# Maxima rows read from PSUM, row sums and gates issued at other places, operand splits in another order, in an attention and gated-unit kernel

## Chip, core and metric

The kernel runs on one core of one Trainium2 chip. Times are device microseconds (us) of that core for one execution. Before the change three runs took 1293.97 to 1294.17 us, with a median of 1294.0.

## The reference

```python
x, g = A_x, sigmoid((A_x * gate_w).sum(-1, keepdims=True))   # 2048 tokens, D = 448
q, k, v = (x @ wqkv).reshape(B, S, 3, 16, 28) ...             # 16 heads of 28 dimensions
a = softmax(q @ k.T * 28 ** -0.5) @ v @ wo
b = (relu(x @ W_gate) * (x @ W_up)) @ W_down                  # F = 1792
return g * a + (1 - g) * b
```

Everything is float32, and the softmax subtracts the maximum of each row.

## The kernel before

**Arithmetic.** TensorE works on float32r tiles. An operand that needs more precision is split into a high part (a copy rounded to float32r: `act_high` on ScalarE, `dve_high` on VectorE) and a low part (what the rounding left, a subtraction: `low` on VectorE, `pool_low` on GpSimd, called POOL here). A product over the 448 input dimensions (three chunks of 128 and one of 64) is then a sum of 11 matmuls, the list `TERMS`: pairs of a plane of the weights (0 to 2 high, 3 to 5 low, 6 both parts of the last chunk) and a chunk of the activations (0 to 3 high, 4 to 7 low). `BY_CHUNK` and `HIGH_FIRST` are the same 11 terms in other orders; in the latter the terms with high weights come first.

**Order of the work.** The schedule is manual: every engine runs its instructions in the order in which the program issues them. Each engine's queue is in order, and so are the queues of DMA issues, those of SyncE (SP) for loads and those of POOL for stores and small reshapes. An instruction at the head of a queue that waits for a semaphore holds up what stands behind it.

**Phase 1, up to some 145 us.** X (activations, transposed) and W (the q, k, v weights) are loaded in blocks and split. `split_first` (line 234) splits weight block 0 and X_0 chunk by chunk: high part of W, high part of X, low part of W, low part of X, for chunks 0 to 3. `split_w` (220) splits a later block of 224 weight columns, which holds two units of 128-column-wide results (its view has an axis `j` of four heads), and `split_x` (266) splits a later block of 512 tokens in two pieces of two chunks. `qk(tb, c)` (300) computes one unit of Q and K: 11 matmuls, then ScalarE's high part of the result and, in the inner function `send`, VectorE's low part and a DMA of both to memory. `send` is called at once, but for the last unit, (0, 6): its `send` is kept and runs at the letter "l" of the first round. That unit's result goes into the second half of the tile `pair`, the raw first gate weights into its first half; those are split into `wg` by `split_f` ahead of the first round. `vproj` computes V and the gate logits `zt`.

**Phase 2, some 145 to 1065 us.** There are 32 rounds of eight key tiles, two for each of the 16 heads. The first of a head is called even, the second odd. A string of letters gives a round's order on TensorE (`FIRST`, `LONG`, `WIDE`, `LATE`):

- "s": a score matmul (tile `s`), and ScalarE's exponential of it into `P`; in the last three rounds two matmuls and one exponential;
- "m": two matmuls of K and Q into a PSUM pair `sm`, and VectorE's maximum over it into a column of `mx`. 32 of them give the row maxima of a head ahead of its turn;
- "x": one of the 11 terms of a gate or up unit (`gu`), "h" a last term; at its end `relu` on ScalarE or the product `h` on VectorE.

The round ends with the split of the next gate weights (`split_f`: ScalarE, POOL) and with `pv` (496), the product of the probabilities and V, 32 matmuls into a PSUM tile `po` of tag "mx", that of the `sm` pairs. The even round's `po` is copied to `os` by ScalarE, the odd round's is added to it by VectorE, and a DMA from POOL reshapes the 2048 row sums into `ls`.

An odd round (and, for head 0, one place in phase 1) begins with `smax_end(h)` (159): TensorE transposes the maxima into a PSUM tile `mt` of tag "x" (two buffers, shared with the `gu` units); ScalarE copies it to `mr` and rounds `mr` into `mh[:, 0]`; VectorE takes the low part; two DMAs issued by POOL write the two as rows 112 and 113 of `Q[h]`, where K has rows of -1, so that the score matmul subtracts the maximum.

`small_things` (554) runs at the start of a round and again behind its 16th score (with the even round's start as quarter 0, so the middle of the even round is quarter 1, the start of the odd one quarter 2). For the head before, quarter 1 issues `row_sums` (VectorE's reciprocal of `ls` into `rs`, a POOL DMA to memory, `l_d`) and `spread` (four POOL DMAs that read `l_d` back, broadcast to `rb`); quarter 2 issues `normalise` (VectorE multiplies `os` by `rb`, four POOL DMAs write `o_d`). The first round's quarter 1 issues `gates` (the sigmoid: an exponential on ScalarE, three VectorE operations).

**Phase 3.** After the last `po` the remaining gate and up units, the output projection (`wo`, with the split weights `WO`) and the down projection (`acc`, weights `WD`). `split_wo` (546) is issued between the last two rounds; `row_sums`, `spread` and `normalise` of head 15 are placed among the first gate units and down products.

## Time and profile before

| | |
|---|---|
| median of three runs | 1294.0 us |
| profiled execution | 1294.1 us, its span 1292.3 |
| TensorE matmuls (PE) | 1285.5 us busy, 99% of the span |
| weight loads (PEld) | 923.7 us, 71% |
| VectorE (DVE) | 808.6 us, 63% |
| ScalarE (ACT) | 749.2 us, 58% |
| GpSimd (POOL) | 366.9 us, 28% |
| granted TensorE clock | 0.9 or more of full speed in every fortieth of the span |

The time of an execution is a little longer than the span of its profile. PE and PEld are two rows of the same engine: the next matmul's weights are loaded while the last one runs, so a weight load that waits (its idle time is given with what ended it) is where TensorE's wait for another engine is seen. Rows of a group have the line, the engine, the operation, the tiles out and in, the count, the busy time and the mean, and then the idle time ahead of them with its releaser. Rows of the timeline and of the chain begin with the start and the length in us.

### The profile page before, as it was taken

Reading aid. Unit: us, or ns where it says so; the run is one execution under the profiler, and the core shown is the slowest. Engines: PE = TensorE matmul, PEld = TensorE weight load, DVE = VectorE, ACT = ScalarE, POOL = GpSimd, SP = SyncE. Lnnn points to the kernel's source line nnn. Section 1 sums busy time; section 2 is a strip of 40 time slices with the busy share of each in tenths; the row PEclk is TensorE's granted clock in tenths of the full one; section 3 lists DMA queues with packets and bytes.
Section 4 is the critical chain, followed back from the end, with each engine's and each line's share of the span. In section 5 each row is a group of like instructions: output and inputs, shape, how many; then the busy total and the mean of one; then the engine's idle time right before and its main releaser. Section 6 shows DMA issues by size and latency. Waiting matters only on the chain.

```text
span 1292.3 us, 17710 instructions
## 1 busy us (share of the span) xinstructions
PE 1285.5 (99%) x6687; PEld 923.7 (71%) x6687; DVE 808.6 (63%) x834; ACT 749.2 (58%) x1402; POOL 366.9 (28%) x551
## 2 busy tenths in 40 slices
PE   9999999999999999999999999999999999999998
PEld 6888766666666666666666666666666656899997
DVE  6487866666777676777766667777777212663342
ACT  5212766666667667676766666767676765322121
POOL 3222132332313222222223332313132353641020
PEclk9999999999999999999999999999999999999999
DMA  9846524151427223241535142432341224644432
GB/s 313 293 156 235 143 87 99 58 129 47 117 63 190 77 78 90 59 99 49 139 101 127 50 114 65 107 70 78 81 132 42 81 87 141 201 136 147 135 110 78
DMA packets 53565, 148.87 MB, mean 115 GB/s; under 512 B 10024, under 2 KB 17128, under 8 KB 48872
## 3 DMA queue, kind: packets, MB, share of 16 engines
q1 hardware_dynamic: 36120, 98.34, 29.1%
q0 software_dynamic: 16928, 48.93, 10.6%
q8 instruction: 53, 0.87, 0.3%
q10 hardware_dynamic: 432, 0.46, 0.1%
q14 instruction: 32, 0.26, 0.1%
HBM read 102.06 MB, written 46.02 MB: 115 GB/s over the span
## 4 chain that ended last, share of the span: by engine, by line
PE 94%; issue 2%; DMA 1%; POOL 1%; ACT 1%; DVE 0%; SPq 0%; ACTq 0%; POOLq 0%
PE gu L468 21%; PE sm L152 18%; PE po L503 16%; PE s L178 16%; PE acc L712 11%; PE qk L303 5%; PE v L321 3%; PE wo L668 3%; PE s L189 2%; DMA ls<-os 1%; POOL wg L99 1%; DMA wr<-wq 0%; PE mt L162 0%; ACT wg L90 0%; ACT WO L90 0%
## 5 line engine op out<-in xcount | busy, mean ns | idle before, releaser
L154 DVE TENSOR_REDUCE mx<-sm 128x1 f32<-128x1024 f32 x512 | 611.1, 1221 | 85.5 <-PE sm L152 85.1
L180 ACT ACTIVATE P<-s 128x512 f32<-128x512 f32 x724 | 401.3, 596 | 174.3 <-PE s L178 164.2
L468 PE MATMUL gu<-X,wg 128*128 128x512 f32 (+1 forms) x1232 | 422.3, 401 | 0.2 <-ACT wg L90 0.2
L178 PE MATMUL s<-Q,K 114*128 114x512 f32 x932 | 364.4, 398 | 0.0
L152 PE MATMUL sm<-K,Q 112*128 112x512 f32 x1024 | 322.4, 396 | 0.3 <-DVE mx L154 0.3
L468 PEld LDWEIGHTS gu<-X,wg 128*128 128x128 f32 (+1 forms) x1232 | 226.5, 189 | 63.7 <-issue 13.8
L152 PEld LDWEIGHTS sm<-K,Q 112*128 112x128 f32 x1024 | 193.5, 190 | 43.9 <-DVE mx L154 4.1
L178 PEld LDWEIGHTS s<-Q,K 114*128 114x128 f32 x932 | 176.2, 189 | 54.4 <-issue 10.1
L503 PE MATMUL po<-P,V 128*32 128x512 f32 x1600 | 181.0, 594 | 0.0
L490 POOL DMA_DIRECT2D h_d<-h x56 | 31.5, 563 | 519.5 <-DVE h L484 455.7
L99 POOL TENSOR_TENSOR wg<-wgr,wg 128x384 fp32r<-128x384 f32 x204 | 146.3, 735 | 8.1
L180 ACT ACTIVATE V<-s 128x512 f32<-128x512 f32 x208 | 115.1, 596 | 45.6 <-PE s L178 43.4
L712 PE MATMUL acc<-WD,hh 128*128 128x448 f32 x672 | 140.9, 368 | 0.0
L712 PEld LDWEIGHTS acc<-WD,hh 128*128 128x128 f32 x672 | 126.1, 188 | 12.9
L503 PEld LDWEIGHTS po<-P,V 128*32 128x32 f32 x1600 | 49.5, 110 | 111.5 <-issue 106.4
L90 ACT ACTIVATE hh<-hr 128x512 fp32r<-128x512 f32 x56 | 35.2, 631 | 119.5 <-PE acc L712 119.5
L96 DVE TENSOR_TENSOR hh<-hr,hh 128x512 fp32r<-128x512 f32 x56 | 46.1, 824 | 64.2 <-ACT hh L90 64.2
L303 PE MATMUL qk<-X,W 128*128 128x512 f32 x308 | 79.6, 399 | 0.4 <-DVE X L96 0.2
L303 PEld LDWEIGHTS qk<-X,W 128*128 128x128 f32 x308 | 58.4, 190 | 15.3 <-DVE X L96 0.7
L90 ACT ACTIVATE wg<-wgr 128x384 fp32r<-128x384 f32 x165 | 66.3, 490 | 3.8 <-DMA wgr<-wgu 2.6
L509 DVE TENSOR_TENSOR os<-po,os 128x512 f32<-128x512 f32 x16 | 11.1, 692 | 91.2 <-PE po L503 91.2
L96 DVE TENSOR_TENSOR mh<-mr,mh 16x128 fp32r<-16x128 f32 x16 | 5.9, 368 | 91.5 <-ACT mh L166 91.5
(73 smaller groups left out, 759.5 us busy)
## 6 DMA issues: line engine op xcount, KB each, us to landing
wgr<-wgu SPq DMA_DIRECT2D x55, 512.0 KB
K<-qk_d SPq DMA_DIRECT2D x64, 224.0 KB
Q<-qk_d SPq DMA_DIRECT2D x64, 224.0 KB
h_d<-h POOLq DMA_DIRECT2D x56, 256.0 KB, 2.3
hr<-h_d SPq DMA_DIRECT2D x56, 256.0 KB
qk_d<-st POOLq DMA_DIRECT2D x21, 512.0 KB, 3.7
x_d<-X POOLq DMA_DIRECT2D x6, 1024.0 KB, 5.1
X<-x_d SPq DMA_DIRECT2D x24, 256.0 KB
```

The lines of the kernel that those rows point to most:

```text
L90: nc.scalar.activation(dst, src, AF.Copy)
L96: nc.vector.tensor_tensor(dst, src, f32(high), op=OP.subtract)
L99: nc.gpsimd.tensor_tensor(dst, src, f32(high), op=OP.subtract)
L152: nc.tensor.matmul(ps[:, c, :], Q[h][:GD, u * P:(u + 1) * P], K[h % 3][:GD, k0:k0 + TB], start=True, stop=True)
L154: nc.vector.tensor_reduce(MX[h][:, 2 * u + half:2 * u + half + 1], ps, axis=AX.XY, op=OP.max)
L178: nc.tensor.matmul(ps, K[h % 3][:GD + 2, kt * P:(kt + 1) * P], Q[h][:GD + 2, j * TB:(j + 1) * TB], start=True, stop=True)
L180: nc.scalar.activation(PT[i][:, j], ps, AF.Exp, scale=SCALE)
L303: nc.tensor.matmul(ps, W[:, a, c * P:(c + 1) * P], xf(tb, b), start=(n == 0), stop=(n == NT - 1))
L321: nc.tensor.matmul(ps[:, :VC], xf(tb, b)[:, t * P:(t + 1) * P], W[:, a, 2 * D:], start=(n == 0), stop=(n == NT - 1))
L468: nc.tensor.matmul(ps, WS[i][rows, s, a], xf(i // NF, b)[rows], start=(n == 0), stop=(n == NT - 1))
L503: nc.tensor.matmul(po[32 * j:32 * j + 32], V[:, h // 4 % 2, i % NK, h % 4], p[:, j], start=(i == i0), stop=(i == i0 + ni - 1))
L712: nc.tensor.matmul(ACC[i // NF][t][:, :D], HH[i][:, a, t * P:(t + 1) * P], WD[:, f, b], start=(f == 0 and n == 0), stop=(f == NF - 1 and n ...
```

## The change

- `smax_end`: `mr` is gone. ScalarE rounds the PSUM tile `mt` directly into `mh[:, 0]`, and VectorE's low part reads PSUM too. The low part and the two POOL DMAs become a function `rest` that the caller runs: in a round behind its first "m", in the late rounds at once, in phase 1 at once.
- `split_first`: the groups are now W and X of chunk 0, W and X of chunk 1, W of chunks 2 and 3, X of chunks 2 and 3.
- `split_w`: of block 1 the columns of the first unit (`j` = 0) are split ahead of the others. The unit (0, 1) uses `HIGH_FIRST`. `split_x` takes the last two chunks of X_1 one at a time.
- `qk`: ScalarE's high part moves into `send`. That changes the order for the last unit alone, where `send` runs later than the splits of the gate weights.
- `gates` moves from the middle of the first round to the end of the second, ahead of `pv`. `row_sums` and `spread` move from the middle of the even round to the start of the odd one, `normalise` from the start of the odd round to its end, ahead of `pv`.
- `split_wo`: the high parts are made by VectorE in place of ScalarE.

```diff
@@ -160,13 +160,15 @@
 
         pt = ps_x(f"mt_{h}")
         nc.tensor.transpose(pt[:16, :P], M.pop(h), ident)
-        mr = keep.tile([16, P], F32, name=f"mr_{h}", tag="mr", bufs=1)
         mh = keep.tile([16, 2, P], F32R, name=f"mh_{h}", tag="mh", bufs=1)
-        nc.scalar.activation(mr, pt[:16, :P], AF.Copy)
-        nc.scalar.activation(mh[:, 0], mr, AF.Copy)
-        low(mh[:, 1], mr, mh[:, 0])
-        for r in range(2):
-            nc.gpsimd.dma_start(f32(Q[h])[GD + r:GD + r + 1], f32(mh)[:, r])
+        act_high(mh[:, 0], pt[:16, :P])
+
+        def rest():
+            low(mh[:, 1], pt[:16, :P], mh[:, 0])
+            for r in range(2):
+                nc.gpsimd.dma_start(f32(Q[h])[GD + r:GD + r + 1], f32(mh)[:, r])
+
+        return rest
 
     PT = {}
 
@@ -219,31 +221,48 @@
 
         def split_w(wr, c0, c1):
 
-            ways = [(W[:, :, c0:c1], wr)]
+            ways = [[(W[:, :, c0:c1], wr)]]
             if c0 < 2 * D:
                 w, r = (ap.rearrange(f"p c {n} -> p c a j d", a=2, j=4)
                         for ap, n in ((W[:, :, c0:c1], "(j a d)"), (wr, "(a j d)")))
-                ways = [(w[:, :, a], r[:, :, a]) for a in range(2)]
-            for w, r in ways:
-                act_high(w[:, 0:3], r[:, 0:3])
-                low(w[:, 3:6], r[:, 0:3], w[:, 0:3])
-            for w, r in ways:
-                act_high(w[:, 6], r[:, 3])
-                low(w[64:, 6], r[64:, 3], w[64:, 6])
+                ways = [[(w[:, :, a], r[:, :, a]) for a in range(2)]]
+
+                if c0 == 2 * GD:
+                    ways = [[(w[:, :, :, 0], r[:, :, :, 0])], [(w[:, :, a, 1:], r[:, :, a, 1:]) for a in range(2)]]
+            for way in ways:
+                for w, r in way:
+                    act_high(w[:, 0:3], r[:, 0:3])
+                    low(w[:, 3:6], r[:, 0:3], w[:, 0:3])
+                for w, r in way:
+                    act_high(w[:, 6], r[:, 3])
+                    low(w[64:, 6], r[64:, 3], w[64:, 6])
 
         def split_first(wr, xr):
 
             r = wr.rearrange("p c (a j d) -> p c a j d", a=2, j=4)
             w = W[:, :, :2 * GD].rearrange("p c (j a d) -> p c a j d", a=2, j=4)
-            for c in range(4):
-                part = xr[c // 2][2][:, c % 2:c % 2 + 1]
+
+            def weights(c):
                 act_high(w[:, c if c < 3 else 6], r[:, c])
-                act_high(X[0][0][:, c:c + 1], part)
+                yield
                 if c < 3:
                     low(w[:, 3 + c], r[:, c], w[:, c])
                 else:
                     low(w[64:, 6], r[64:, 3], w[64:, 6])
+                yield
+
+            def tokens(c):
+                part = xr[c // 2][2][:, c % 2:c % 2 + 1]
+                act_high(X[0][0][:, c:c + 1], part)
+                yield
                 low(X[0][1][:, c:c + 1], part, X[0][0][:, c:c + 1])
+                yield
+
+            for group in ((weights(0), tokens(0)), (weights(1), tokens(1)), (weights(2), weights(3)),
+                          (tokens(2), tokens(3))):
+                for _ in range(2):
+                    for part in group:
+                        next(part)
 
         def load_x(tb):
             r = []
@@ -265,8 +284,10 @@
 
         def split_x(tb, raw):
             for c0, c1, xr in raw:
-                act_high(X[tb][0][:, c0:c1], xr)
-                low(X[tb][1][:, c0:c1], xr, X[tb][0][:, c0:c1])
+
+                for a, b in ((c0, c0 + 1), (c0 + 1, c1)) if (tb, c0) == (1, 2) else ((c0, c1),):
+                    act_high(X[tb][0][:, a:b], xr[:, a - c0:b - c0])
+                    low(X[tb][1][:, a:b], xr[:, a - c0:b - c0], X[tb][0][:, a:b])
 
         def spill_x(tb, r):
             nc.gpsimd.dma_start(x_d[tb, r], f32(X[tb][r]))
@@ -303,9 +324,9 @@
                 nc.tensor.matmul(ps, W[:, a, c * P:(c + 1) * P], xf(tb, b), start=(n == 0), stop=(n == NT - 1))
                 mix(n, among)
             st = st_tile(tb, c)
-            act_high(st[:, 0], ps)
 
             def send():
+                act_high(st[:, 0], ps)
                 low(st[:, 1], ps, st[:, 0])
                 nc.gpsimd.dma_start(qk_d[:, c * P:(c + 1) * P, tb * TB:(tb + 1) * TB].rearrange("r d t -> d r t"),
                                     f32(st))
@@ -365,7 +386,7 @@
 
         x2 = load_x(2)
         w2 = load_w(2)
-        qk(0, 1)
+        qk(0, 1, HIGH_FIRST)
         split_x(2, x2)
         x3 = load_x(3)
         qk(1, 0)
@@ -420,7 +441,7 @@
             f(*a, among=among)
 
             if 0 in M and ends >= 2 * NK:
-                smax_end(0)
+                smax_end(0)()
         assert m == ahead, m
 
     def gates():
@@ -544,9 +565,9 @@
         return r[:, :, :D]
 
     def split_wo(r):
-        act_high(WO[:, 0:3], r[:, 0:3])
+        dve_high(WO[:, 0:3], r[:, 0:3])
         pool_low(WO[:, 3:6], r[:, 0:3], WO[:, 0:3])
-        act_high(WO[:, 6], r[:, 3])
+        dve_high(WO[:, 6], r[:, 3])
         pool_low(WO[64:, 6], r[64:, 3], WO[64:, 6])
 
     nxt = parts = i0 = 0
@@ -561,15 +582,11 @@
         if u in (16, 32):
             g = u // 16 + 1
             nc.sync.dma_start(V[:, g % 2], v_d[g])
-        if u == 1:
-            gates()
         if u == 2:
             pack_wo()
-        if h and q == 1:
+        if h and q == 2:
             row_sums(h - 1)
             spread(h - 1)
-        if h and q == 2:
-            normalise(h - 1)
 
     split_f(0, act_high, pool_low, (0,))
     fetch_f(1)
@@ -580,8 +597,11 @@
         todo = list(range(nxt, nxt + nu))
         nxt += nu
         small_things(i0 // 4)
+        rest = None
         if m % (2 * NK) == 0 and i0 <= NI - LEAD:
-            smax_end(m // (2 * NK) - 1)
+            rest = smax_end(m // (2 * NK) - 1)
+            if late:
+                rest()
         if late and wor is None:
             wor = load_wo()
 
@@ -603,6 +623,10 @@
             elif o == "m":
                 smax(m)
                 m += 1
+
+                if rest:
+                    rest()
+                    rest = None
             elif o == "x":
                 i, half, n = passes.pop(0)
                 if n == 0:
@@ -635,6 +659,11 @@
             parts += 1
             if parts % 2 == 0:
                 fetch_f(parts // 2 + 1)
+
+        if i0 == NK // 2:
+            gates()
+        if i0 > NK and i0 % NK:
+            normalise(i0 // NK - 1)
         pv(i0, ni)
         i0 += ni
         if late and i0 == NI - NK // 2:
```

## The prediction

> **What bounds the kernel now.** I read the page first, then the chain that ended last in order of time, then the waits, then the timeline at the places where the weight loads (PEld) waited for another engine. The page gives TensorE nearly the whole span:
>
> ```profile
> PE 1285.5 (99%) x6687; PEld 923.7 (71%) x6687; DVE 808.6 (63%) x834; ACT 749.2 (58%) x1402; POOL 366.9 (28%) x551
> ```
>
> A busy TensorE may still lose time between matmuls, so the chain matters more:
>
> ```profile
> 10.33 28.09 PE qk L303 x120
> ...
> 615.48 7.01 PE po L503 x64
> 645.18 7.01 PE po L503 x64
> 675.08 7.01 PE po L503 x64
> ...
> 767.04 7.01 PE po L503 x64
> 797.09 7.01 PE po L503 x64
> ...
> 1098.05 2.48 PE acc L712 x12
> ```
>
> Columns: start, length, what. From 10.33 us the matmuls run at 28.09/120 = 0.234 us each, and the chain stays on TensorE. The starts of the probability-times-V block (`po`) give the length of a round. 615.48 to 645.18, a first-half ("even") round, takes 29.70 us; 645.18 to 675.08, a second-half ("odd") round, which begins with the transposition of the maxima, takes 29.90; the odd round 767.04 to 797.09, one of five of a slower kind, takes 30.05. So the steady part is bound by the number of matmuls, which the change leaves alone, and it can win only the short gaps in front of single matmuls, the start before 10.33, and places where TensorE stands still for one late operation. I call the matmul's own time TensorE's floor; what follows is a list of its exceptions.
>
> **The change, part by part.** The sum is made against the profiled execution, which took 1294.1 us (span 1292.3 and 1.8 around it), 0.1 over the median of 1294.0.
>
> *Start.* Order of the first splits, first part of block 1 ahead of the rest, second unit with its high terms first, last piece of X_1 in two. Timeline of before:
>
> ```profile
> 7.50 0.69 DVE L96 TENSOR_TENSOR X<-xr,X 128x512 fp32r<-128x512 f32 x1 [0.26 <-ACT X L90]
> ...
> 8.64 0.69 DVE L96 TENSOR_TENSOR X<-xr,X 128x512 fp32r<-128x512 f32 x1
> ...
> 8.83 1.23 ACT L90 ACTIVATE W<-wr 128x336 fp32r<-128x336 f32 x4 [0.56 <-DMA wr<-wq]
> 9.35 1.42 DVE L96 TENSOR_TENSOR W<-wr,W 128x336 fp32r<-128x336 f32 x4
> 9.39 0.19 PEld L303 LDWEIGHTS qk<-X,W 128*128 128x128 f32 x1 [0.48 <-DVE X L96]
> ...
> 10.33 27.66 PEld L303 LDWEIGHTS qk<-X,W 128*128 128x128 f32 x120 [0.40 <-DVE W L96]
> ...
> 11.53 2.41 DVE L96 TENSOR_TENSOR X<-xr,X 128x1024 fp32r<-128x1024 f32 x2
> ```
>
> Before, VectorE's queue runs X chunk 2, W chunk 3, X chunk 3, and waits 0.26 us for ScalarE's part of X chunk 2. The W chunk 3 part takes about 0.45 (8.19 to 8.64). After, W chunk 3 stands ahead of both X chunks on both engines: its VectorE part fills the 0.26 wait, and X chunk 3 ends near 9.05 instead of 9.33. The first unit's last matmul starts then, not at 9.39. Block 1 lands as before (ScalarE got it at 8.83). Its first ScalarE part shrinks from 336 to 168 columns, so it ends near 9.15 instead of 9.3, and six terms with high weights now need nothing from VectorE: 6 x 0.234 = 1.4 us, in which the low part (about 0.35 after 9.2) is ready. So the second unit starts near 9.3 and runs through to 9.3 + 11 x 0.234 = 11.9; before, its second term waited until 10.33 and the unit ended at 10.33 + 10 x 0.234 = 12.7. Gain 0.8. Against it: two more operations on ScalarE and VectorE each (about 0.2 us) stand ahead of X_1, whose low parts took VectorE until 11.53 + 2.41 = 13.94. They would now end near 14.3; the third unit wants the last of them at 11.9 + 10 x 0.234 = 14.2. I take 0.1 off: **0.7**; ends 0.25 (only the first unit's part) and 0.95.
>
> *Last qk unit.* Its ScalarE high part moves behind the first split of the gate weights:
>
> ```profile
> 144.37 0.60 ACT L90 ACTIVATE pair<-qk 128x512 fp32r<-128x512 f32 x1
> ...
> 144.60 0.64 PE L178 MATMUL s<-Q,K 114*128 114x512 f32 x2
> 144.85 0.53 ACT L90 ACTIVATE wg<-pair 128x384 fp32r<-128x384 f32 x1
> ...
> 145.43 0.53 PEld L468 LDWEIGHTS gu<-X,wg 128*128 128x128 f32 x3 [0.64 <-ACT wg L90]
> 145.43 0.96 PE L468 MATMUL gu<-X,wg 128*128 128x512 f32 x3 [0.19 <-ACT wg L90]
> ...
> 146.22 0.63 PE L152 MATMUL sm<-K,Q 112*128 112x512 f32 x2
> ```
>
> ScalarE did `pair` (0.60) first, `wg` after it, and the first gate matmul waited. TensorE should have gone on at 144.60 + 2 x 0.234 = 145.07 and went on at 145.43, and lost 0.09 more on restarting (145.43 + 3 x 0.234 = 146.13, the next matmul at 146.22). Together 0.45, at an idle time of the weight loads of 0.64: below I take idle less 0.19 for what the matmuls lose. After, `wg` takes the place of `pair`, half a microsecond earlier, and the wait is gone; `pair` is late next, and only its DMA waits for that. **0.45**; low end 0, should `wg` wait for the memory it takes over.
>
> *Maxima rows from PSUM.* One of two ScalarE copies per head goes (0.25); VectorE's low part and the two POOL DMAs move behind the round's first maximum. The start of the odd round that begins when the `po` block of 767.04 ends (774.05):
>
> ```profile
> 774.61 0.25 ACT L165 ACTIVATE mr<-mt 16x128 f32<-16x128 f32 x1
> ...
> 774.89 0.31 ACT L166 ACTIVATE mh<-mr 16x128 fp32r<-16x128 f32 x1
> ...
> 775.10 2.25 ACT L180 ACTIVATE P<-s 128x512 f32<-128x512 f32 x4
> 775.23 0.42 DVE L96 TENSOR_TENSOR mh<-mr,mh 16x128 fp32r<-16x128 f32 x1 [5.92 <-ACT mh L166]
> ...
> 775.73 0.19 PEld L178 LDWEIGHTS s<-Q,K 114*128 114x128 f32 x1 [0.27 <-ACT P L180]
> ...
> 776.84 0.30 PEld L152 LDWEIGHTS sm<-K,Q 112*128 112x128 f32 x2 [0.33 <-DVE mx L154]
> ...
> 777.49 1.02 POOL L169 DMA_DIRECT2D Q<-mh  x2
> ```
>
> The first exponential starts behind `mr` and `mh`, and the third score matmul's weight load waits 0.27 for it. VectorE's queue stands for 5.92 us at `mh`, with the first maximum behind it, and the third pair of maxima matmuls waits 0.33 for that. After, `mh` starts at 774.61 and the exponential near 774.85, 0.25 earlier, which covers the 0.27 up to the normal gap; and the first maximum is reduced ahead of the low part, so its PSUM is free about 0.4 earlier, over the 0.33. PSUM of the transposition is held until the low part is done, a little over 1 us longer; the next gate unit but one wants it, 11 matmuls later. From the chain, an odd round costs 0.20 more than an even one, one of the slower kind 0.35. The transposition and its load keep some of that; I take 0.10 in each of 14 odd rounds (0.27 - 0.19 = 0.08 from the load's wait; ends 0 and 0.20) and 0.15 more in the five of the slower kind, where the maxima wait too (ends 0 and 0.15): 1.4 + 0.75 = **2.15**; ends 0 and 3.55.
>
> *Row sums, spreading, normalisation.* The same operations, half a round later each. One place shows what that is worth:
>
> ```profile
> 393.92 0.25 DVE L517 RECIPROCAL rs<-ls 128x16 f32<-128x16 f32 x1 [1.68 <-DMA ls<-os]
> ...
> 395.30 0.30 PEld L152 LDWEIGHTS sm<-K,Q 112*128 112x128 f32 x2 [0.72 <-DVE mx L154]
> ```
>
> The reciprocal waited 1.68 for a slow landing of the row sums, with the maxima behind it on VectorE, and TensorE lost 0.72 - 0.19 = 0.53. After, the transfer has half a round more. **0.53**; ends 0 and 0.53. On POOL the order changes: at the start of an odd round now stand the write of the reciprocals, a wait for it to land, four spreading DMAs, and only then the maxima rows for the next head, in place of four output DMAs of 0.51 each (as the two of 1.02 above):
>
> ```profile
> POOL rb L524 <- DMA l_d<-rs: 53.7, 15, 7.2
> ...
> POOL ls L512 <- DVE os L509: 21.8, 8, 3.3
> ```
>
> ```profile
> L528 DVE TENSOR_TENSOR os<-os,rb 128x512 f32<-128x512 f32 x16 | 13.1, 817 | 2.0 <-DMA rb<-l_d 2.0
> ```
>
> Columns of the waits: total, times, longest; of the group: busy, mean ns. The wait for that landing took 53.7/15 = 3.6 us on average, 7.2 at most. So the maxima rows, issued 3.4 us into the round (777.49 against 774.05), go near 3.4 + 0.5 + 3.6 = 7.5, at worst 11.1. The first score that needs them is the 29th of 32 in the round; with 28 scores, 26 or so gate terms and 15 pairs of maxima ahead, it comes (28 + 26 + 30) x 0.234 = 19.7 us into the round. Cost nothing; the cover is 8.5 us or more. The four output DMAs now stand ahead of the row sums' transfer at the end of an odd round. That transfer had waited for VectorE 21.8/8 = 2.7 us, more than the 2.04 of four issues, and is wanted a round later. The multiplication itself (0.82 on average) moves from among the maxima to just behind POOL's weight splits, where the 7.01 of `po` cover it.
>
> *Gates.* One small exponential and three small VectorE operations go to where both engines stand idle beside `po`. Nothing.
>
> *Output weights' high part on VectorE, and the tail:*
>
> ```profile
> 1059.19 6.04 POOL L99 TENSOR_TENSOR wg<-wgr,wg 128x384 fp32r<-128x384 f32 x8
> ...
> 1063.24 1.78 ACT L90 ACTIVATE WO<-wor 128x1344 fp32r<-128x1344 f32 x2
> ...
> 1065.99 0.30 PEld L189 LDWEIGHTS s<-Q,K 114*128 114x128 f32 x2 [1.21 <-ACT V L191]
> ...
> 1095.05 0.25 DVE L517 RECIPROCAL rs<-ls 128x16 f32<-128x16 f32 x1 [0.80 <-DMA ls<-os]
> 1095.42 0.39 DVE L93 CAST WD<-wdr 128x448 fp32r<-128x448 f32 x1
> ...
> 1096.20 1.23 POOL L99 TENSOR_TENSOR WD<-wdr,WD 128x448 fp32r<-128x448 f32 x1
> ```
>
> ScalarE's 1.78 us of WO held up the exponentials, and the scores lost 1.21 - 0.19 = **1.02**. VectorE has nothing to do there (no maxima in the last three rounds). WO has 4 x 448 columns a partition; at the 0.39 of the cast of 448 above, 1.56 us of casts. Its rival for memory is POOL:
>
> ```profile
> L93 DVE CAST WD<-wdr x14: 382/392/3841, 1095.4 to 1155.5; 128x448 fp32r<-128x448 f32 x14
> ```
>
> The same cast of 448 columns took 0.38 at least and 3.84 at most, beside POOL's own splits. So the casts and POOL's `wg` parts (6.04 us for eight, the first done by 1059.95) may delay each other by 1.56 or more. Even then the first `wg` part is there by 1061.5, while the gate matmuls begin after `po`, near 1063. I take 0; ends 0 and 1.56. The Trainium skill, page "SBUF — State Buffer", section "Who interferes with whom", says that a VectorE copy in its two-port mode and a GpSimd instruction shut each other out for whole instructions. The trace agrees (0.38 against 3.84), and by that rule alone the sum below would be smaller by up to 1.56, if POOL's parts were needed at once.
>
> In the tail the last normalisation of head 14 puts its 2.04 us of DMA issues ahead of the row sums of head 15. Their reciprocal (1095.05, already 0.80 late) stands ahead of the first cast of WD; POOL's part ended at 1097.43, and the first down matmul that reads it is the second of the last block in the chain, at 1098.05 + 2.48/12 = 1098.26. Cover 0.83, slip 0 to 2.0. By the 2.7 above most of it falls into POOL's wait: **-0.1**; ends 0 and -1.2.
>
> **Sum.** 0.7 + 0.45 + 2.15 + 0.53 + 1.02 - 0.1 = 4.75 us. 1294.1 - 4.75 = 1289.35; less 0.1 for the median, **1289.3 us**. Lower end with all upper ends (0.95 + 0.45 + 3.55 + 0.53 + 1.02 = 6.5): 1287.5. Upper end with the start at 0.25, no gain in the rounds, and the tail at -1.2 (0.25 + 0.45 + 0.53 + 1.02 - 1.2 = 1.05): 1292.9.
>
> **The rivals.** (A) *The round starts give nothing*: another wait is there when `mr` is gone, the copy of `po` on ScalarE ahead of it or the low part between two maxima. For it: `mh` still waits for the transposition. Against it: even rounds, which lack only this work, are 0.20 shorter. Time 1289.3 + 2.15 = 1291.4. (B) *Slower: maxima rows come too late.* Place: POOL at the start of odd rounds. It decides once the write of the reciprocals takes some 8.5 us longer than the mean 3.6; then each of 14 rounds loses the excess, and 3 us each make +42: 1331. Against it: the longest such wait was 7.2. (C) *The casts hold POOL for their whole length and TensorE waits*: 1289.3 + 1.56 = 1290.9. (D) *The change does nothing*: the waits removed were each followed by another as long: 1294. Against it: each wait above has a named releaser that goes.
>
> **Chances.** The forecast 0.64, with a range of its own of 1288.2 to 1290.8; A 0.16; C 0.05; rounds at their upper end (1287.9) 0.04; D 0.04; B and other losses 0.07. Faster by over 0.2% (below 1291.4; 0.2% is about what a measurement here can tell from no change): 0.64 + 0.05 + 0.04 and a third of A, 0.78. Within 0.2%: the rest of A and D, 0.15. Slower: 0.07. Half of A, D and B lie outside 1287.5 to 1291.6, some 0.2.
>
> **What would show it.** Right: the steady run of `qk` matmuls begins near 9.3; no wait of `gu` for `wg` near 145; odd rounds between `po` blocks near 29.80, all alike; no wait of `sm` for `mx` near 394; no gap of scores near 1065. Wrong: odd rounds still at 29.90 (A); weight loads of `s` waiting for the maxima rows' DMA in the last quarter of odd rounds (B); a down matmul waiting for WD near 1098 (tail).

## The result and the profile after

The changed kernel takes 1289.61 us (median of seven runs, 1289.47 to 1289.90) against 1293.85 for the one before (seven runs): a ratio of 0.9968, 95% interval 0.9956 to 0.9980, or 4.24 us less. The forecast was 1289.3. Its profiled execution has a span of 1287.8 us, 4.5 shorter than the one before. The busy shares, from the page after:

```profile
PE 1281.6 (100%) x6687; PEld 926.6 (72%) x6687; DVE 809.7 (63%) x839; ACT 743.2 (58%) x1387; POOL 365.9 (28%) x551
```

TensorE's busy time fell with the span; no engine's load moved by more than 6 us. The chain of the kernel after (start, length, what):

```profile
158.82 7.00 PE po L524 x64
166.78 1.24 DVE mx L154
189.72 7.00 PE po L524 x64
...
613.60 7.01 PE po L524 x64
643.30 7.01 PE po L524 x64
673.04 7.01 PE po L524 x64
...
764.79 7.01 PE po L524 x64
794.51 7.01 PE po L524 x64
```

An even round (613.60 to 643.30) still takes 29.70. An odd round now takes 29.74 (643.30 to 673.04; before 29.90), and those of the slower kind 29.72 (764.79 to 794.51; before 30.05). But the first odd round takes 30.90 (158.82 to 189.72), and a maximum on VectorE stands in the chain there. The same two starts in the kernel before, 30.16 apart:

```profile
159.67 7.00 PE po L503 x64
189.83 7.01 PE po L503 x64
```

TensorE runs the same 6687 matmuls in the same order in both kernels, so the start of each can be compared with that of its twin, the same matmul in the other trace. Every place where the difference between the two steps is a wait that went (plus) or came (minus). The table has the steps of more than 0.05 us:

| place | forecast, us | step in the traces, us |
|---|---|---|
| start, up to the third unit | 0.70 | 0.66 |
| first gate matmul, behind `wg` | 0.45 | 0.45 |
| a maxima pair 3 us later | 0 | -0.22 |
| first odd round (LONG, head 1) | 0.25 | -0.75 |
| first exponential, 13 other odd rounds | 1.30 | 1.38 (0.10 to 0.115 each) |
| maxima pair, the four other rounds of the slower kind | 0.60 | 0.68 (0.17 each) |
| reciprocal behind the row sums | 0.53 | 0.55 |
| scores behind WO | 1.02 | 1.04 |
| tail | -0.1 | 0 |
| sum | 4.75 | 3.79 |

The other 0.7 us between the spans comes in steps of under 0.05. It lies in the odd rounds too: 29.90 to 29.74 is 0.16 and 30.05 to 29.72 is 0.33, each some 0.06 more than its steps in the table. From `po` to `po` the thirteen odd rounds behind the first are 2.9 us shorter in all, against 1.38 + 0.68 in the table. The even rounds, phase 1 behind its start and phase 3 have nothing of it, and the granted clock was 1.00 in both profiles from 10 to 1285 us, so it is not the clock.

Three rows of the table are not as forecast: the maxima pair, the first odd round and the tail. I give the lines of the two that lost. Timeline of the kernel after at the first gate matmul (start, length, engine, line, operation, tiles; in brackets the idle time and what ended it):

```profile
144.14 0.60 ACT L90 ACTIVATE pair<-qk 128x512 fp32r<-128x512 f32 x1
144.32 0.55 PEld L489 LDWEIGHTS gu<-X,wg 128*128 128x128 f32 x3 [0.16 <-ACT wg L90]
...
145.98 0.68 DVE L96 TENSOR_TENSOR pair<-qk,pair 128x512 fp32r<-128x512 f32 x1
...
146.57 3.48 DVE L154 TENSOR_REDUCE mx<-sm 128x1 f32<-128x1024 f32 x3
...
147.84 0.30 PEld L152 LDWEIGHTS sm<-K,Q 112*128 112x128 f32 x2 [0.39 <-DVE mx L154]
```

The gate matmul's load waits 0.16 in place of 0.64. But VectorE's low part of the last unit (145.98) still stands among the maxima, TensorE is now 0.45 further on, and a maxima pair at 147.84 waits 0.39 for VectorE. Timeline at the start of the first odd round:

```profile
166.10 0.64 PE L152 MATMUL sm<-K,Q 112*128 112x512 f32 x2
...
166.38 0.25 ACT L90 ACTIVATE mh<-mt 16x128 fp32r<-16x128 f32 x1
...
166.78 1.23 DVE L154 TENSOR_REDUCE mx<-sm 128x1 f32<-128x1024 f32 x1 [6.23 <-PE sm L152]
...
167.92 0.27 DVE L96 TENSOR_TENSOR mh<-mt,mh 16x128 fp32r<-16x128 f32 x1
168.06 0.30 PEld L152 LDWEIGHTS sm<-K,Q 112*128 112x128 f32 x2 [1.28 <-DVE mx L154]
168.06 0.73 PE L152 MATMUL sm<-K,Q 112*128 112x512 f32 x2 [0.86 <-DVE mx L154]
```

The first maxima pair runs at 166.10, is reduced from 166.78 to 168.01, and only then does the second start, 0.86 late by the matmul's row and 1.01 against its normal distance. In the kernel before, the second of these pairs starts 0.94 behind the first, without a wait:

```profile
166.96 0.64 PE L152 MATMUL sm<-K,Q 112*128 112x512 f32 x2
...
167.90 0.63 PE L152 MATMUL sm<-K,Q 112*128 112x512 f32 x2
```

### The profile page after: what moved, and what is told of

Same layout as the page of the kernel before. It is cut to its first block, busy times and chain, and to the rows that moved or that the text cites. A ratio compares the mean times of both kernels' runs of the same rounds, so it can differ in the third digit from the quotient of the medians.

```text
span 1287.8 us, 17721 instructions
## 1 busy us (share of the span) xinstructions
PE 1281.6 (100%) x6687; PEld 926.6 (72%) x6687; DVE 809.7 (63%) x839; ACT 743.2 (58%) x1387; POOL 365.9 (28%) x551
## 4 chain that ended last, share of the span: by engine, by line
PE 99%; DVE 0%; ACT 0%; issue 0%
PE gu L489 22%; PE sm L152 19%; PE po L524 17%; PE s L180 17%; PE acc L741 11%; PE qk L324 6%; PE v L342 3%; PE wo L697 3%; PE s L191 2%; PE warm_ps L369 0%; PE mt L162 0%; DVE mx L154 0%; DVE y L747 0%; ACT V L346 0%; DVE warm L366 0%
## 5 line engine op out<-in xcount | busy, mean ns | idle before, releaser
L505 DVE TENSOR_TENSOR h<-gu,rl 128x512 f32<-128x512 f32 x56 | 38.7, 692 | 28.0 <-ACT rl L502 23.0
```

What stands on the lines that cost most here:

```text
L505: nc.vector.tensor_tensor(h, ps, RL.pop(i), op=OP.mult)
```

## The experiments

The ratios' intervals are some 0.0012 wide on either side, 1.5 us, so medians alone cannot carry differences of a few tenths. Each verdict below goes by the median and by the steps against the twin trace together. Gains are against the kernel before, measured beside each run.

| run | median, us | gain, us | ratio, 95% interval |
|---|---|---|---|
| changed kernel | 1289.61 | 4.24 | 0.9968 (0.9956 to 0.9980) |
| buffers in turn | 1288.52 | 5.26 | 0.9960 (0.9948 to 0.9973) |
| low part at once | 1288.27 | 5.51 | 0.9958 (0.9946 to 0.9971) |
| `mr` back | 1291.30 | 2.48 | 0.9981 (0.9972 to 0.9990) |
| `pair` first | 1289.72 | 4.06 | 0.9970 (0.9958 to 0.9981) |
| WO on ScalarE | 1290.43 | 3.28 | 0.9974 (0.9964 to 0.9984) |
| row sums early | 1289.70 | 4.01 | 0.9969 (0.9957 to 0.9981) |
| start as before | 1290.23 | 3.48 | 0.9971 (0.9959 to 0.9982) |
| low part at once, "l" later | 1289.27 | 4.44 | 0.9964 (0.9952 to 0.9977) |
| first block as before | 1289.77 | 3.91 | 0.9969 (0.9957 to 0.9980) |
| gates as before | 1289.90 | 3.78 | 0.9969 (0.9958 to 0.9981) |
| rows 8 us later | 1297.06 | -3.38 | 1.0025 (1.0014 to 1.0035) |
| rows 12 us later | 1328.59 | -34.91 | 1.0265 (1.0251 to 1.0279) |

### Why the first odd round lost

PSUM, the memory that the matmuls write to, has numbered banks; the part of the build that gives tiles their memory is called the planner here. In the built programs, the banks of the wide tiles around this place are:

```
before   sm_63: 6   po_0: 4   sm_64: 6   sm_65: 4   sm_66: 6
after    sm_63: 6   po_0: 4   sm_64: 6   sm_65: 6   sm_66: 4
```

The tag "mx" has two buffers, and they go to 603 tiles. Before, they alternate throughout. After, they alternate everywhere but here: the first two maxima pairs of head 1 share a buffer, so the second has to wait until the first is reduced. The first run takes the buffers strictly in turn.

```diff
+    wide = [0]
...
-        return psum.tile([P, 2, TB], F32, tag="mx", bufs=2, name=name)
+        wide[0] += 1
+        return psum.tile([P, 2, TB], F32, tag=f"mx{wide[0] % 2}", bufs=1, name=name)
```

> The changed kernel with the two wide PSUM buffers taken strictly in turn. Theory (the first odd round loses its time because its first two pairs of maxima got one and the same PSUM buffer, so the second waits for the first to be reduced): the wait of 1.0 us and the 0.1 of restarting behind the first maximum of that round go, the second pair starts about 0.95 us after the first, and the kernel gains 5.3 us on the one before (about 1288.5). Rival (VectorE itself is late there, whichever buffer is used): the wait stays, the gain stays at 4.2.

Timeline of this run, the first two maxima pairs and the reduction between them:

```profile
166.61 0.64 PE L155 MATMUL sm<-K,Q 112*128 112x512 f32 x2
...
167.28 1.23 DVE L157 TENSOR_REDUCE mx<-sm 128x1 f32<-128x1024 f32 x1 [6.23 <-PE sm L155]
...
167.55 0.63 PE L155 MATMUL sm<-K,Q 112*128 112x512 f32 x2
```

The second pair starts 0.94 after the first and does not wait for the reduction. Against the changed kernel the twin steps are +1.01 and +0.11 at this place, and none above 0.05 elsewhere but in the start. The gain is 5.26, as the theory had it; the rival is out.

The low part was put off behind the first maximum. The second run issues it at once in every round.

```diff
-            if late:
-                rest()
+            rest()
+            rest = None
```

> The changed kernel with the low part of the maxima and its two DMAs issued at once in every round, ahead of the first maximum. Theory (reading PSUM directly is what helps; putting the low part off is worth nothing): all odd rounds stay as short as in the changed kernel, no pair of maxima waits at the start of the five slower rounds, and, since the buffers alternate again in this build, the first odd round is 1.1 us shorter: gain of about 5.3 us on the kernel before. Rival (the deferral carries the 0.17 us of each of the slower odd rounds, as the prediction had it): these come back in four or five rounds, gain about 4.5.

Gain 5.51. Here too the steps are +1.01 and +0.11 in the first odd round, since the buffers of this build alternate, and no other step above 0.05 after the start: the four rounds of the slower kind keep their gain. So the deferral is worth nothing and is what made the planner hand out the buffers differently. That the planner hands out the buffer that it expects to be free first is what I suppose; no run shows its reckoning.

The third run restores ScalarE's copy alone.

```diff
-        act_high(mh[:, 0], pt[:16, :P])
+        mr = keep.tile([16, P], F32, name=f"mr_{h}", tag="mr", bufs=1)
+        nc.scalar.activation(mr, pt[:16, :P], AF.Copy)
+        act_high(mh[:, 0], mr)
...
-            low(mh[:, 1], pt[:16, :P], mh[:, 0])
+            low(mh[:, 1], mr, mh[:, 0])
```

> The changed kernel with ScalarE's copy of the transposed maxima restored, the low part still put off. Theory (the copy alone held the exponentials, 0.107 us in each odd round): 13 times 0.107 come back, gain on the kernel before 4.2 - 1.4 = 2.8 us; the slower rounds keep their 0.17. Rival (the low part's place ahead of the maxima also made the first exponential late): less than 0.4 us comes back.

Starts of `po` in this run's chain:

```profile
615.32 7.01 PE po L526 x64
645.03 7.01 PE po L526 x64
...
674.92 7.01 PE po L526 x64
```

The odd round (645.03 to 674.92) is back at 29.89, 0.15 longer than the changed kernel's 29.74. The twin steps are 13 times 0.100 to 0.108, 1.35 in sum, all at the matmul behind the second score; smaller steps right behind them make up the rest of the 0.15, and the slower rounds' 0.17 does not come back. The gain is 2.48: 1.8 lost by the medians, 1.9 behind the start in the traces. So the copy by itself is worth 0.15 in each odd round, more than the theory's 0.107, and for the maxima of the slower rounds either edit alone is enough. The low part is still put off in this build, and `sm_64` and `sm_65` again share bank 6: against the run with the low part at once the first odd round loses 1.02 and 0.11. So it is the deferral, with the copy or without it, that brings the shared buffer. What the missing copy does is seen in the kernel after, at the odd round that begins at 771.80:

```profile
772.36 0.25 ACT L90 ACTIVATE mh<-mt 16x128 fp32r<-16x128 f32 x1
772.52 1.07 ACT L182 ACTIVATE P<-s 128x512 f32<-128x512 f32 x2
...
773.90 0.27 DVE L96 TENSOR_TENSOR mh<-mt,mh 16x128 fp32r<-16x128 f32 x1
...
779.52 0.98 POOL L169 DMA_DIRECT2D Q<-mh  x2
```

The exponential follows `mh` at 772.52, 0.16 after it began, where before it stood behind two operations.

### The last unit and the gates

```diff
             st = st_tile(tb, c)
+            act_high(st[:, 0], ps)

             def send():
-                act_high(st[:, 0], ps)
```

> The changed kernel with ScalarE's high part of the last unit back ahead of the gate weights' split. Theory (half of that edit's 0.45 us is given back at the third pair of maxima of the first round, since VectorE's queue does not move with TensorE): the wait of the first gate matmul, 0.45 us, is back, and the wait of the maxima pair some 3 us later, 0.22 us, is gone: 0.23 us lost, gain on the kernel before 4.0. Rival (that second wait has another cause): 0.45 lost and the second wait stays, gain 3.8.

Gain 4.06. The steps are -0.36 and -0.10 at the gate matmul (its load waits 0.64 again), +0.12 and +0.10 at the maxima pair three microseconds on. So half of this edit's 0.45 is indeed paid back by VectorE's queue. The next run gives the gates back to the first round.

```diff
+        if u == 1:
+            gates()
...
-        if i0 == NK // 2:
-            gates()
```

> The changed kernel with the gates' exponential and three VectorE operations back in the first round. Theory (they take 0.6 us of VectorE, but its queue there has recovered by then): nothing lost that can be measured, gain 4.2 us. Rival (VectorE is behind TensorE in that whole round, as the wait of the third pair of maxima shows): 0.2 to 0.6 us lost, gain 3.6 to 4.0.

Timeline of this run:

```profile
148.71 0.47 DVE L450 TENSOR_SCALAR e<-e 128x16 f32<-128x16 f32 x1
...
150.85 0.30 PEld L152 LDWEIGHTS sm<-K,Q 112*128 112x128 f32 x2 [0.52 <-DVE mx L154]
```

The steps are -0.25 and -0.10, at a maxima pair (150.85) that waits 0.52 behind these small operations; gain 3.78. The rival is right: VectorE has no slack in the first round, and having the gates elsewhere is worth 0.35 us to the changed kernel (0.46 by the medians).

Since the low part of the last unit costs 0.22, I tried it later (the letter "l" moves behind the third "m"), together with the edit above that issues the low part of the maxima at once.

```diff
-FIRST = "s" * 12 + "mmlssxxxmsxsxuxmsxm...
+FIRST = "s" * 12 + "mmssxxxmsxsxluxmsxm...
```

> The changed kernel with the low part of the maxima at once (as in the run that did this alone, gain 5.5) and the last unit's high and low parts sent later, just ahead of the second split of the first gate weights, behind the third maximum of the round in place of the second. Theory (the wait of 0.22 us of the maxima pair comes from VectorE's 0.68 us low part among closely spaced maxima): the wait moves to the next pair or two and shrinks to about 0.1, gain 5.6. Rival (VectorE has no slack in that whole stretch): 0.2 or more is waited a little later, gain 5.3 to 5.5.

```profile
146.72 0.60 ACT L90 ACTIVATE pair<-qk 128x512 fp32r<-128x512 f32 x1
...
147.35 0.69 DVE L96 TENSOR_TENSOR pair<-qk,pair 128x512 fp32r<-128x512 f32 x1 [0.43 <-ACT pair L90]
...
148.35 0.73 POOL L331 DMA_DIRECT2D qk_d<-pair  x1 [3.20 <-DVE pair L96]
...
150.70 0.19 PEld L489 LDWEIGHTS gu<-X,wg 128*128 128x128 f32 x1 [0.94 <-POOL wg L99]
```

Both missed: gain 4.44, 1.1 less than without this edit. ScalarE's `pair` at 146.72 now stands right ahead of the second half of `wg`, and on POOL the DMA of `pair` (148.35) stands ahead of the low part of `wg`, which so begins only at 149.11. A gate matmul's load waits 0.94 for that at 150.70, 0.78 in the steps. Another 0.52 goes just before, at a score and at a maxima pair near 149, and 0.24 comes back at the pair that had waited. The unit's place was better where it was.

### The output weights

```diff
-        dve_high(WO[:, 0:3], r[:, 0:3])
+        act_high(WO[:, 0:3], r[:, 0:3])
...
-        dve_high(WO[:, 6], r[:, 3])
+        act_high(WO[:, 6], r[:, 3])
```

> The changed kernel with the high parts of the output weights back on ScalarE. Theory (ScalarE's 1.8 us ahead of the exponentials was the whole loss, and VectorE's casts cost TensorE nothing, although they took 3.2 us beside POOL's splits): the wait of the paired scores near 1061 us is back, 1.04 us lost, gain on the kernel before 3.2. Rival (the casts on VectorE hold up POOL's splits and with them something later): part of the 1.04 comes back elsewhere, gain above 3.5.

This run's timeline, and then the kernel after: VectorE's timeline, POOL's, and the duration of the casts (ns, minimum, median, maximum):

```profile
1060.44 1.78 ACT L90 ACTIVATE WO<-wor 128x1344 fp32r<-128x1344 f32 x2
...
1063.19 0.30 PEld L191 LDWEIGHTS s<-Q,K 114*128 114x128 f32 x2 [1.21 <-ACT V L193]
```

```profile
1054.71 3.18 DVE L93 CAST WO<-wor 128x1344 fp32r<-128x1344 f32 x2
```

```profile
1055.65 6.09 POOL L99 TENSOR_TENSOR wg<-wgr,wg 128x384 fp32r<-128x384 f32 x8
```

```profile
L93 DVE CAST WO<-wor x2: 1544/1630/1717, 1054.7 to 1056.2; 128x1344 fp32r<-128x1344 f32 x1, 128x448 fp32r<-128x448 f32 x1
```

The steps of the run are -0.94 and -0.10, both at the paired scores; gain 3.28. The 1.04 is the whole of it. In the kernel after the two casts take 3.18 us, twice the 1.56 that I had reckoned. The second (448 columns) falls wholly beside POOL's `wg` parts and takes 1.72, against the 0.38 of the same cast of WD at its fastest; POOL's eight parts take 6.09, against 6.04 before. So the casts waited for POOL, and POOL not for them, and nothing behind the casts was needed soon. The Trainium skill, page "SBUF — State Buffer", section "Who interferes with whom", has it that the order of issue decides which of the two is blocked, for a whole instruction. The trace agrees with the lock (1.72 against 0.38). It does not show the order deciding: POOL's first part began at 1055.65, within the first cast (1054.71 to 1056.25), and took 1.02, as it did before. That POOL could be the one blocked, no run here shows.

### The row sums

```diff
-        if h and q == 2:
+        if h and q == 1:
             row_sums(h - 1)
             spread(h - 1)
+        if h and q == 2:
+            normalise(h - 1)
...
-        if i0 > NK and i0 % NK:
-            normalise(i0 // NK - 1)
```

> The changed kernel with row sums, spreading and normalisation half a round earlier again, as before the change. Theory (one slow landing of the row sums cost 0.55 us in the kernel before, and half a round more covers it): the reciprocal waits again for the row sums of at least one head, and 0.5 us is lost: gain 3.7. Rival (that landing was slow by chance in one execution): no wait of the maxima behind the reciprocal, gain 4.2.

```profile
380.99 0.74 POOL L533 DMA_DIRECT2D ls<-os  x1 [3.31 <-DVE os L530]
...
392.57 0.25 DVE L538 RECIPROCAL rs<-ls 128x16 f32<-128x16 f32 x1 [1.26 <-DMA ls<-os]
```

The slow landing is no accident: at the same head the row sums, issued at 380.99, are again waited for until 392.57, 1.26 us of it on VectorE (1.68 before). But TensorE lost only one step of 0.10, where it had lost 0.55, and the gain is 4.01. The wait recurs, and both sides had part of it: it cost 0.55 in one execution and 0.10 in the other. That the two buffers of the maxima absorb the difference is what I suppose.

### The start

```diff
-            for group in ((weights(0), tokens(0)), (weights(1), tokens(1)), (weights(2), weights(3)), ...
+            for c in range(4):     # W and X chunk by chunk
...
-                if c0 == 2 * GD:   # first unit's columns of block 1 first
-                    ways = ...
...
-                for a, b in ((c0, c0 + 1), (c0 + 1, c1)) if (tb, c0) == (1, 2) else ((c0, c1),):
...
-        qk(0, 1, HIGH_FIRST)
+        qk(0, 1)
```

> The changed kernel with all splits of the start as before. Theory (the order of the splits gives 0.65 us): gain on the kernel before 4.2 - 0.65 = 3.6 us. Rival (the first loads land at times that scatter by half a microsecond from one execution to the next, and the order matters little): gain 4.0 to 4.2.

Gain 3.48, 0.76 less than the changed kernel's; the theory holds. The next run restores the order of the first block alone (the first of the four pieces above).

> The changed kernel with the first block's splits (W and X_0, chunk by chunk) in the order of before; the other three edits of the start stay. Theory (the prediction's: that order is worth the 0.35 us by which the first unit's last matmul came later, the rest of the start's gain is the second unit's): 0.35 us lost, gain on the kernel before 3.9. Rival (the second unit's wait is what counts, and it hides the first unit's): gain 4.2. Second rival (all of the start's 0.65 us hangs on it): gain 3.6.

Gain 3.91, 0.33 less, but the median says little: three of the six times lie near 1289.5 and three near 1290.1. The trace says more. The first unit's last two matmuls come 0.18 and 0.36 later, as they do in the run before, less 0.09 and 0.07 that the second and third unit get back. That bears out the theory, 0.35 for the order of the first block and the rest for the second unit, whose rows in the kernel after are

```profile
8.97 1.42 ACT L90 ACTIVATE W<-wr 128x168 fp32r<-128x168 f32 x6 [1.06 <-DMA wr<-wq]
9.05 5.05 PEld L324 LDWEIGHTS qk<-X,W 128*128 128x128 f32 x22 [0.30 <-DVE X L96]
9.35 1.80 DVE L96 TENSOR_TENSOR W<-wr,W 128x168 fp32r<-128x168 f32 x6 [0.35 <-ACT W L90]
```

The load at 9.05 waits 0.30 for the first unit's last low part (9.39 before), and the 22 loads from there run on without a wait through the second unit. ScalarE got block 1 at 8.97 and VectorE its first piece at 9.35, well before the terms that need low weights.

### How late may the maxima rows be?

The slower rival (B) needed a price. 16 and 24 small DMA issues more on POOL delay the rows; nothing is left out of the computation, and the small transfers go to memory that nothing reads.

```diff
             nc.gpsimd.dma_start(LS[h][32 * j:32 * j + 32], l_d[h][j:j + 1].to_broadcast([32, TB]))
+        if h < H - 2:
+            for k in range(16):    # 24 in the second run
+                nc.gpsimd.dma_start(dram.tile([P, 16], F32, name=f"idle_{h}_{k}"), ident[:, :16])
...
+            rest()                 # the low part at once
```

> The changed kernel with the low part at once (alone: gain 5.5 us), and 16 small DMAs more issued by POOL between the spreading of the reciprocals and the maxima rows: 16 x 0.5 = 8 us of delay. Theory (the rows, issued 7.7 us into an odd round and 2.9 us more in issuing and landing, are wanted 20.1 us into it, so the cover is 9.5 us): nothing lost, gain 5.5. Rival (the rows are already close to late, or what stands behind them on POOL is): several us lost in each of 13 rounds, 20 us and more in all.

In the kernel after the rows go at 779.52 in the round that begins at 771.80, 7.7 us into it (forecast 7.5). With 8 us more, twelve of the thirteen odd rounds before the last three rounds show no step above 0.05 and one loses 0.81; that much agrees. But by the medians 8.8 us are lost against the run with the low part at once, and 7.5 of them lie in one place in the traces: the odd round with the late order. Its rows in the kernel after, then in this run, then what TensorE waited for there (total, times, longest) and three stretches of this run (length, busy time of PE, PEld, DVE, ACT, POOL, then the granted clock, DMA share and GB/s):

```profile
1017.39 0.98 POOL L169 DMA_DIRECT2D Q<-mh  x2
```

```profile
1027.40 0.99 POOL L169 DMA_DIRECT2D Q<-mh  x2
1029.66 0.50 PEld L191 LDWEIGHTS s<-Q,K 114*128 114x128 f32 x2 [5.95 <-issue]
```

```profile
PE s L191 <- DMA Q<-mh: 5.5, 1, 5.5
```

```profile
1024.00:1030.00 6.00, 0.46 (x2) 0.34 (x2) 0.00 (x0) 0.57 (x1) 4.39 (x9) 0.73 0.07 14
1030.00:1036.00 6.00, 6.00 (x32) 3.21 (x35) 1.90 (x3) 3.86 (x7) 0.22 (x1) 0.70 0.02 4
```

```profile
1029.70:1033.60 3.90, 3.90 (x10) 2.67 (x12) 0.00 (x0) 1.94 (x2) 0.00 (x0) 0.50 0.00 0
```

The rows go at 1027.40, and the score that needs them has its weights at 1029.66; against its twin that matmul is 5.7 us late. This round begins at 1009.55 in the kernel after and, by the steps up to there, 0.66 earlier here, so the rows go 7.8 and 18.5 us into it. The cover was 18.5 - 7.8 - 5.7, some 5 us, and not the 8.5 of the other rounds, since the late order asks for the next head's scores sooner. Another 1.8 us go in the steps right after the stall: the granted clock was 0.50 for the first 3.9 us of work, 0.70 over the whole stretch from 1030 to 1036. The Trainium skill, page "TensorE: Matmul & The Clock Gate", section "Part 1: The HAM clock gate", says that the clock halves after an idle window of about 3.4 us; the stall of 5.7 us and the 0.50 agree with it.

> As the run with 8 us, with 24 small DMAs: 12 us of delay, 2.8 us more than the cover in the eleven odd rounds with the shorter order, 0.7 us in the two with the longer one, and about 3 us in the late one. Theory: 11 x 2.8 + 2 x 0.7 + 3 = 35 us lost against the run that only has the low part at once, about 1323 us, with score matmuls waiting for the rows' DMA in the last quarter of odd rounds. Rival (the cover is larger than that): under 10 us lost.

1328.59, 40.3 above the run with the low part at once; 35 were expected. What TensorE waited for in this run (total, times, longest):

```profile
PE s L180 <- DMA Q<-mh: 20.4, 10, 4.1
PE s L191 <- DMA Q<-mh: 8.8, 1, 8.8
```

Ten odd rounds wait 2.0 us on average for the rows and the late one 8.8, together 29.2. Most of the other 11 us are slower matmuls: at five of the waits the granted clock went to 0.50, for 27 us in all, of which TensorE worked for some 19 and so lost 9 to 10. Three of these waits left TensorE idle for about 4 us or more, but two for 2.1 and 2.4 only, while three more of 1.9 to 2.4 did not bring the clock down. So here an idle time of about 3.4 us is not needed, and the measurement differs from that rule of the Trainium skill. Rival B's mechanism is real, and what kept it away is the distance: the rows would have to come some 5 us later in the late round, or about 8 and more in the others.

## Why the prediction was right

The sum was right within 0.5 us of the medians' difference. Most of its steps held; three did not. That the sum came so near is in part luck, since two errors of 1 us each cancel in its largest term. (The chances count from an upper end of 1291.6, while the sum gives 1292.9; no working leads to the smaller figure.)

*Start, 0.70:* 0.66 in the trace, and the run with the old start lost 0.76. Right, its split into first and second unit too, by the steps of both runs. The first unit's end (9.05) came as worked out, and block 1 landed 0.14 later (8.97). One trace alone would not carry this, since the start scatters by up to 1 us (see the end).

*Last unit, 0.45:* the wait went as said, but "`pair` is late next, and only its DMA waits for that" failed. VectorE's low part of `pair` is not covered: it sits between maxima that TensorE needs, and gave 0.22 back.

*Maxima rows, 2.15:* by the lengths of the rounds 2.15 too, and that is luck: the thirteen odd rounds gave 2.9 where the forecast had 1.9, and the first gave -0.75 where it had 0.25. Right was 0.15 more for the rounds of the slower kind (0.17 in four). Too small was 0.10 for each odd round: "The transposition and its load keep some of that" took half of the 0.20 away, but an odd round is now only some 0.04 longer than an even one, and the copy alone was worth 0.15. The step that failed is "the first maximum is reduced ahead of the low part, so its PSUM is free about 0.4 earlier". The deferral brought nothing that the missing copy did not bring alone, and in the first odd round it changed which PSUM buffer the second maxima pair gets: -0.75 for +0.25. I had followed instructions and queues through the change, but not the assignment of buffers, which an order of instructions does not show.

*Row sums, 0.53:* 0.55 in the trace, 0.2 by the medians of the run that moves them back. The slow landing was rightly taken as something that recurs; its price was read from one execution. The cover of the maxima rows, 8.5 us or more, was right in twelve rounds, about 1 too large in a thirteenth (0.81 lost at 8 us), and wrong for the late one, some 5 us, for which I had not counted the scores.

*Gates, nothing:* there is no step of its own in the traces of before and after, but the move was not worth nothing. In the changed kernel, where TensorE is ahead of VectorE in the first round, the gates at their old place cost 0.35. The engines stand idle where the gates went to, which I had looked at, but VectorE was busy where they came from, which I had not. What the move alone would do for the kernel before, no run shows.

*WO, 1.02:* 1.04. Rival C's lock was there (3.18 us of casts), on the other side: POOL lost nothing.

*Tail, -0.1:* 0. Rivals A and D are out by the 13 odd rounds.

## What to carry to other kernels

Where TensorE is busy 99%, the few tenths left lie in front of single matmuls; comparing the start of each with its twin in the other trace turns a difference of 0.3% into a list of named waits. A threshold on the steps hides what lies under it, though: 0.7 us came in steps of under 0.05, and only the lengths of the rounds showed where. When an edit moves an instruction on one engine, look also at which buffers the planner then gives out: two neighbours that share a buffer cost 1.1 us here, and taking the buffers in turn got it back (the best version, with the low part at once, takes 1288.27, ratio 0.9958). For every operation that is moved, look at the place that it leaves as well as the one it goes to.

## What the runs showed of the hardware

The start scatters more than expected: in eleven profiled executions whose start is that of the changed kernel, the same matmul some 139 us into the kernel begins anywhere from 138.97 to 140.01, and the steps between them all lie before 15 us, where operations wait for the first loads. A line of an execution that starts late, that of the run with WO on ScalarE:

```profile
7.04 0.67 ACT L90 ACTIVATE W<-wr 128x224 fp32r<-128x224 f32 x2 [0.91 <-DMA wr<-wq]
```

In the kernel after no ScalarE operation on W waits at that place. A comparison of two single profiles is uncertain by up to 1 us for that reason alone. A stall of TensorE can cost more than its length: 5.7 us of waiting were followed by 3.9 us of work at a granted clock of 0.50, which cost 1.8 more.
